# Slot sums in three pieces, row sums ahead of the second layer, and fewer half-width pieces at the end of a pooled-attention and soft-MoE kernel

## The chip, the cores and the metric

The kernel runs on one core of one Trainium2 chip. A core has TensorE (PE in the profile; its weight loads are PEld), VectorE (DVE), ScalarE (ACT), GpSimd (POOL) and SyncE (SP), which work side by side and wait for one another through semaphores, and 16 DMA engines that all queues share. The metric is the device time in microseconds; lower is better.

## The reference

Queries, keys and values have 8 batches, 8 heads, 576 tokens and 64 columns. Keys and values are averaged over 8 neighbouring tokens (72 remain), and ordinary softmax attention follows. Its output, 4608 tokens of 512 columns, goes through a soft mixture of 8 experts with 4 slots each:

```python
logits = x @ phi                       # 4608 x 32
d = softmax(logits, over the tokens)
slot_input = d.T @ x                   # 32 slots x 512
for e in range(E):
    h = np.maximum(slot_input[e] @ w1[e], 0.0)    # 4 x 1024
    slot_out[e] = h @ w2[e]                       # 4 x 512
c = softmax(logits, over the slots)
return c @ slot_out                    # 4608 x 512, float32
```

`w1` and `w2` have 16.8 MB each, the output has 9.4 MB. Both softmaxes use the same exponentials, divided once by sums over tokens and once by sums over slots.

## The kernel before

**Attention.** The batches go in four pairs. POOL issues all loads in an order written out by hand, and they are cast to bf16 on the way. For each pair the scores of a head are one `score_unit` (line 301): two matmuls into the bank pair `sc`, one exponential on ACT into `exa`. A `u_tile` (311) handles 128 tokens of four heads (one of two `qd`): its matmuls write the unnormalised attention output, the head's share of the logits and the row sum into `u_ps`; DVE inverts the sum (`rec`) and DVE, or ACT with `by_scalar`, writes the normalised result into `xsa`. A pair has nine such tiles (t = 0 to 8) for each `qd`. `u_ps` has two buffers, so the matmuls of a tile wait until the tile before last is normalised. Until the attention closes, a scheduler orders PE, ACT and DVE; only POOL's order is by hand. Behind `att.close()` (503) all engines follow the order of the code.

**Slot sums.** `dispatch` (334) sums the logits over heads (on PE with an identity, or on DVE for the last pair), takes the exponentials `ee` on ACT, and adds nine matmuls, one for each tile t, into `G_ps`. `add_up` adds the pairs into `G`, and for the last pair into `Gb`. `turn` (355) transposes the exponentials into `cT`, which the combination with the experts' outputs needs. For pairs 0 to 2 this lies beside the next pair's attention. For the last pair (lines 471 to 478) nothing is left beside it.

**Experts.** `hidden` (514) multiplies the slots with `w1` into `h_ps`, `turn_hidden` transposes `h` into `hT`. The inverse `recC` of the sums over tokens is made on DVE, and with it `hz`, `z_ps` and `zT`: a shortcut by which the very last row group of `w2` reaches the first two output tiles without waiting for `so`. `second_layer` (538) adds products of `hT` with row groups j = 0 to 7 of `w2` for each expert into `so_ps`. `row_sums` (403) computes the sums over slots as matmuls of `cT` with one-hot columns, copies them to SBUF on ACT, and turns them into `recR`. `busy(n)` (568) multiplies something that nobody reads (`idle_ps`).

**w2.** Experts 0 to 5 and row groups 0 to 2 of expert 6 are loaded in full width. The rest (13 row groups: five of expert 6, eight of expert 7) is loaded in column halves, first all left halves, then all right halves (487 to 495), into `xsa`, which the last pair's tokens leave free. `PIECES` (92) lists them.

**Output.** Tokens are written in groups of 2, 2, 2, 4, 6, 8 and 12 rows a partition (`GROUPS`, 57); a row is an output tile of 128 tokens. `begin(half)` (611) scales `so_ps` by `recC` into `so_a` and `so`, and makes tiles 0 and 1; `tiles` (624) makes more tiles of one half and stores them. Ten tiles are made by halves. The left half is done while the right half's weights still arrive. Tiles 10 to 35 are made in full width, ACT and DVE taking turns, and stored by whole groups through SP.

Of the kernel before, what the change touches and what calls it, by code (L numbers as in the profile page):

```python
# [18 lines left out]
def kernel(  # L19
# [36 lines left out]
    GROUPS, base = [], 0  # L56
    for rows in (2, 2, 2, 4, 6, 8, 12):
        GROUPS.append((rows, base))
        base += 128 * rows
# [28 lines left out]

    CUT6 = FJ - 5
    HC = DM // 2  # L90
# [219 lines left out]

    def u_tile(pair, qd, t, ex, by_scalar=False):

        ps = ps_u.tile([128, HQ, XW + 1], FP, name="u_ps", tag="u")
        for hh in range(HQ):
            for b in range(2):
                if t < 8 and b != t // 4:
                    continue
                c = (t % 4 if t < 8 else 4) * 128
                rows = slice(0, 128) if t < 8 else slice(b * 64, (b + 1) * 64)
                nc.tensor.matmul(out=ps[rows, hh],  # L320
                                 lhsT=ex[b][:, hh].rearrange("p r t -> p (r t)")[:, c:c + rows.stop - rows.start],
                                 rhs=vp[(2 * pair + b) % 5][:, qd * HQ + hh, 0:XW + 1],
                                 start=True, stop=True)
        rec = small.tile([128, HQ], FP, name="rec", bufs=3)
        nc.vector.reciprocal(out=rec, in_=ps[:, :, XW])  # L325
        dst = xs[pair][:, t, qd * HQ:(qd + 1) * HQ, :]
        if by_scalar:
            for hh in range(HQ):
                nc.scalar.activation(out=dst[:, hh], in_=ps[:, hh, 0:XW], func=AF.Copy, scale=rec[:, hh:hh + 1])
        else:  # L330
            nc.vector.tensor_tensor(out=dst, in0=ps[:, :, 0:XW],  # L331
                                    in1=rec.rearrange("p h -> p h ()").to_broadcast([128, HQ, XW]), op=ALU.mult)

    def dispatch(x, ps, ee, by_vector=False):

        if by_vector:
            lg = small.tile([128, 9, NS], FP, name="lg", bufs=1)
            nc.vector.reduce_sum(out=lg, in_=x[:, :, :, D:XW].rearrange("p t h c -> p t c h"), axis=AX.X)  # L338
        else:
            lg = ps_m.tile([128, 9, NS], FP, name="lg_ps", tag="m")  # L340
            for h in range(H):
                nc.tensor.matmul(out=lg, lhsT=ident, rhs=x[:, :, h, D:XW], start=(h == 0), stop=(h == H - 1))
        nc.scalar.activation(out=ee, in_=lg.rearrange("p t s -> p t () s").to_broadcast([128, 9, NG, NS]), func=AF.Exp)  # L343
        yield
        for t in range(9):
            nc.tensor.matmul(out=ps, lhsT=ee[:, t].rearrange("p g s -> p (g s)"), rhs=x[:, t, :, 0:D],  # L346
                             start=(t == 0), stop=(t == 8))
# [23 lines left out]
    def combine(pair):  # L371

        ps = ps_m.tile([128, DM], FP, name="G_ps", tag="m")
        ee = small.tile([128, 9, NG, NS], BF, name="ee", bufs=1)
        parts = dispatch(xs[pair], ps, ee)
        next(parts)
        yield
        next(parts, None)
        add_up(pair, ps, G)
# [19 lines left out]
    for c, (n, t) in enumerate(quads + rest):  # L399
        for i in range(2 * t.shape[1]):  # L400
            place[n + i] = (i, c)

    def row_sums():

        ps = ps_m.tile([NC, 4, 128], FP, name="R_ps", tag="m")
        for c, (_, t) in enumerate(quads + rest):
            nc.tensor.matmul(out=ps[:, 0:2 * t.shape[1]].rearrange("p (s r) i -> p s r i", r=2),   # L407
                             lhsT=onehot[:, MAXC - 1 - c:MAXC - 1 - c + NC], rhs=t,
                             start=(c == 0), stop=(c == NC - 1), skip_group_check=True)
        sums = consts.tile([NC, 4, 128], FP)  # L410
        nc.scalar.copy(out=sums, in_=ps)
        ps = ps_m.tile([128, 4, NC], FP, name="RT_ps", tag="m")
        for i in range(4):
# [24 lines left out]
    for pair in range(NP):  # L438
        for qd in range(2):
# [5 lines left out]
            for i in range(9):  # L445
# [5 lines left out]
                else:  # L451
                    u_tile(pair, qd, i - 5, ex)
                step(prep)
# [124 lines left out]
    so = post.tile([128, DM], BF)  # L578

    out_a = exf.rearrange("p (n c) -> p n c", c=DM)  # L580
    out_b = w1f.rearrange("p (n c) -> p n c", c=DM)
    n = 0
    places = []
    for rows, base in GROUPS:
        home = out_a[:, n:n + rows] if n + rows <= 6 else out_b[:, n - 6:n - 6 + rows]
        places.append((home, out[base:base + 128 * rows].rearrange("(p r) c -> p r c", r=rows)))
        n += rows
# [44 lines left out]
    for e in range(4):  # L632
        second_layer(e)
    row_sums()
    busy(512)
# [20 lines left out]
    tiles(4, 6, 1)  # L656
    tiles(6, 10, 1)
    for n in range(10, len(TILES)):
        g, r = TILES[n]
# [33 lines left out]
```

## Time and profile before

| | us |
|---|---|
| median of 3 runs (lowest, highest) | 175.68 (175.49, 175.91) |
| span of the profiled execution, first to last instruction | 179.6 |
| PE, DVE, ACT busy | 129.9, 97.1, 88.3 |
| last score exponentials end, `Gb` starts | 110.6, 128.59 |
| loads end, first store issued | 148.3, 152.40 |
| last store issued, landed | 167.5, 178.3 |

For the profiled execution only the span is given, with profiling running; the runs had none. A line of the chain of waits is one link of the work that ended last: start, duration, engine, tile written, line of code, count of instructions. A line of windows gives the busy time of each engine in one stretch, then the clock granted to TensorE (1.00 is full), the share of the 16 DMA engines, and the bytes moved. The share can pass 1, since packets overlap in the records.

### The profile page before, as it was taken

How to read it: one execution, taken by the hardware profiler on the slowest of the kernel's cores; microseconds unless marked ns; L12 is line 12 of the kernel's file. 1: busy time of each engine (PE TensorE's matmuls, PEld its weight loads, DVE VectorE, ACT ScalarE, POOL GpSimd, SP SyncE). 2: the span in 40 equal slices, each digit the busy share in tenths (PEclk: the TensorE clock that was granted, in tenths of full speed). 3: DMA queues.
4: the chain of work that ended last, by engine and by line, in shares of the span. 5: the costliest groups of instructions: out<-in, count | busy, mean ns of one | idle time of the engine just before them, and what ended most of it. 6: DMA issues, size and time to landing. Idle time of an engine off the chain costs nothing.

```text
span 179.6 us, 2853 instructions
## 1 busy us (share of the span) xinstructions
PE 129.9 (72%) x1106; PEld 70.2 (39%) x1106; DVE 97.1 (54%) x258; ACT 88.3 (49%) x168; POOL 19.9 (11%) x37
## 2 busy tenths in 40 slices
PE   0006888999899999999998996512996988798000
PEld 0002463565555655556555543300443232333000
DVE  5403353387868588785888629764335000599200
ACT  3201238986887649876599726232012012799100
POOL 7000111052100040000100004000700300000000
PEclk9999999999999999999999669655559999999755
DMA  5999999999999999999999999999999990699995
GB/s 197 242 209 233 207 220 216 213 224 203 204 220 216 216 207 220 225 204 219 208 230 204 221 217 210 228 206 223 214 210 207 196 181 7 225 342 428 480 394 235
DMA packets 10780, 41.13 MB, mean 229 GB/s; under 512 B 768, under 2 KB 6656, under 8 KB 7184
## 3 DMA queue, kind: packets, MB, share of 16 engines
q0 software_dynamic: 7440, 30.48, 83.9%
q1 hardware_dynamic: 3328, 10.49, 15.0%
q8 instruction: 8, 0.13, 0.3%
q14 instruction: 4, 0.03, 0.0%
HBM read 61.93 MB, written 9.44 MB: 397 GB/s over the span
## 4 chain that ended last, share of the span: by engine, by line
PE 51%; ACT 17%; DVE 14%; DMA 6%; issue 3%; POOL 1%; DVEq 0%; ACTq 0%; POOLq 0%
PE pool_ps L234 9%; ACT exa L308 7%; DMA phi_f<-in_moe_phi_dram 6%; PE G_ps L346 6%; PE sc L306 6%; PE u_ps L320 6%; PE q_ps L266 5%; DVE w_sb L575 4%; PE h_ps L521 3%; DVE xsa L331 3%; PE so_ps L542 3%; ACT vmeans L240 2%; DVE lg L338 2%; PE R_ps L407 2%; PE turn_ps L250 2%
## 5 line engine op out<-in xcount | busy, mean ns | idle before, releaser
L308 ACT ACTIVATE exa<-sc 72x576 bf16<-72x576 f32 x64 | 39.5, 652 | 5.1 <-PE sc L306 4.3
L331 DVE TENSOR_TENSOR xsa<-u_ps,rec 128x384 bf16<-128x384 f32 x69 | 37.4, 554 | 1.3
L320 PE MATMUL u_ps<-vp,exa 72*128 72x97 bf16 (+1 forms) x320 | 27.3, 217 | 4.5 <-DVE xsa L331 3.7
L320 PEld LDWEIGHTS <-exa 72*128 72x128 bf16 (+1 forms) x320 | 18.2, 104 | 16.0 <-DVE xsa L331 6.8
L306 PE MATMUL sc<-qTa,kp 64*72 64x288 bf16 x128 | 22.0, 309 | 1.9 <-ACT exa L308 1.5
L234 PE MATMUL pool_ps<-big,pmat 128*128 128x512 bf16 x64 | 18.6, 411 | 0.7 <-ACT qTa L270 0.6
L325 DVE RECIPROCAL rec<-u_ps 128x4 f32<-128x4 f32 x72 | 11.5, 172 | 12.8 <-PE u_ps L320 12.6
L346 PE MATMUL G_ps<-xsa,ee 128*128 128x512 bf16 x36 | 12.0, 496 | 6.6 <-ACT ee L343 6.6
L266 PE MATMUL q_ps<-ident,big 128*128 128x128 bf16 x144 | 12.5, 231 | 0.2
L186 PE MATMUL phi_ps<-spread,sel 128*128 128x256 bf16 x4 | 1.3, 397 | 15.1 <-DVE spread L181 15.1
L600 PE MATMUL f_ps<-so,cT 128*128 128x512 bf16 (+1 forms) x42 | 10.2, 337 | 1.8 <-ACT w_sb L573 0.8
L306 PEld LDWEIGHTS <-kp 64*72 64x72 bf16 x128 | 8.0, 108 | 8.3 <-issue 3.1
L575 DVE TENSOR_SCALAR w_sb<-f_ps,recR 128x512 f32<-128x512 f32 (+1 forms) x17 | 10.5, 683 | 0.4 <-PE f_ps L600 0.2
L266 PEld LDWEIGHTS <-big 128*128 128x128 bf16 x144 | 9.6, 104 | 2.4 <-issue 0.7
L242 DVE TENSOR_REDUCE rsum<-rest_ps 128x64 f32<-128x512 f32 x8 | 5.5, 692 | 9.3 <-PE rest_ps L238 9.2
L270 ACT COPY qTa<-q_ps 128x768 bf16<-128x768 bf16 x8 | 6.3, 794 | 7.8 <-PE q_ps L266 7.8
L272 DVE COPY qTa<-q_ps 128x768 bf16<-128x768 bf16 x16 | 8.8, 553 | 2.1 <-PE q_ps L266 2.0
L573 ACT ACTIVATE w_sb<-f_ps,recR 128x512 f32<-128x512 f32 (+1 forms) x17 | 9.6, 638 | 0.5 <-PE f_ps L600 0.3
L492 POOL DMA_DIRECT2D xsa<-in_moe_w_dram x8 | 6.0, 754 | 26.2 <-PE G_ps L346 15.3
L346 PEld LDWEIGHTS <-ee 128*128 128x128 bf16 x36 | 4.1, 120 | 12.3 <-ACT ee L343 6.8
L234 PEld LDWEIGHTS <-pmat 128*128 128x128 bf16 x64 | 5.8, 103 | 6.4 <-issue 2.3
L240 ACT CAST vmeans<-pool_ps 128x1024 bf16<-128x1024 f32 x4 | 4.0, 1012 | 6.8 <-PE pool_ps L234 6.8
(104 smaller groups left out, 155.1 us busy)
## 6 DMA issues: line engine op xcount, KB each, us to landing
w_sb<-in_moe_w_dram POOLq DMA_DIRECT2D x2, 3072.0 KB, 37.2
big<-in_q_dram POOLq DMA_DIRECT2D x4, 1152.0 KB, 12.0
big<-in_v_dram POOLq DMA_DIRECT2D x4, 1152.0 KB, 15.8
big<-in_moe_w_dram POOLq DMA_DIRECT2D x1, 4096.0 KB, 40.0
big<-in_k_dram POOLq DMA_DIRECT2D x3, 1152.0 KB, 21.4
out_dram<-w_sb SPq DMA_DIRECT2D x1, 3072.0 KB, 10.8
qTa<-in_moe_w_dram POOLq DMA_DIRECT2D x1, 2048.0 KB, 30.4
out_dram<-w_sb SPq DMA_DIRECT2D x1, 2048.0 KB, 7.5
```

The source lines that it names most:

```text
L234: nc.tensor.matmul(out=ps, lhsT=pmat, rhs=src[:, t:full * POOL:POOL, :], start=(t == 0), stop=(t == POOL - 1))
L266: nc.tensor.transpose(out=ps[:, t].rearrange("p n i -> p (n i)"), in_=q_sb[pair][:, tt:tt + 2, :].rearrange("p t d -> p (t d)"), identity= ...
L272: nc.vector.tensor_copy(out=dst, in_=ps)
L306: nc.tensor.matmul(out=ps[:, r, 0:S // 2], lhsT=kp[pair][rows, n], rhs=qT[pair][rows, n].rearrange("p t i -> p (t i)"), start=True, stop=True)
L308: nc.scalar.activation(out=dst.rearrange("p r (i t) -> p r i t", t=NU), in_=ps[:, :, 0:S // 2].rearrange("p r (t i) -> p r i t", i=NI), fu ...
L320: nc.tensor.matmul(out=ps[rows, hh], lhsT=ex[b][:, hh].rearrange("p r t -> p (r t)")[:, c:c + rows.stop - rows.start], rhs=vp[(2 * pair + ...
L325: nc.vector.reciprocal(out=rec, in_=ps[:, :, XW])
L331: nc.vector.tensor_tensor(out=dst, in0=ps[:, :, 0:XW], in1=rec.rearrange("p h -> p h ()").to_broadcast([128, HQ, XW]), op=ALU.mult)
L346: nc.tensor.matmul(out=ps, lhsT=ee[:, t].rearrange("p g s -> p (g s)"), rhs=x[:, t, :, 0:D], start=(t == 0), stop=(t == 8))
L573: nc.scalar.activation(out=dst, in_=src, func=AF.Copy, scale=by)
L575: nc.vector.tensor_scalar(out=dst, in0=src, scalar1=by, scalar2=None, op0=ALU.mult)
L600: nc.tensor.matmul(out=ps, lhsT=tokens(n), rhs=so[:, cols], start=True, stop=True)
```

## The change

1. For the last pair, the logits go through PE (`weigh`) and the slot sums (`gather`) in three pieces: tiles 0 to 3, 4 to 6 and 7 to 8. DVE's reduction of the logits is gone. Tiles 1, 3, 5 and 7 of the last half pair are normalised on ACT, where it was 4, 6 and 8. Tiles 6, 7 and 8 are written into the free score banks (`spare`) instead of `u_ps`.
2. `row_sums` is split: its ten matmuls and the copy move ahead of `z_ps`, and `turn_sums` with the inverses stays behind the first four experts. Three more `busy(512)` follow there.
3. `CUT6` goes from 3 to 7: seven row groups of expert 6 are loaded whole, and one of expert 6 and eight of expert 7 by halves.
4. `GROUPS` becomes 2, 2, 4, 6, 8, 14, and eight tiles are made by halves.

```diff
-    for rows in (2, 2, 2, 4, 6, 8, 12):
+    for rows in (2, 2, 4, 6, 8, 14):
...
-    CUT6 = FJ - 5
+    CUT6 = 7
...
-    def u_tile(pair, qd, t, ex, by_scalar=False):
-
-        ps = ps_u.tile([128, HQ, XW + 1], FP, name="u_ps", tag="u")
+    def u_tile(pair, qd, t, ex, by_scalar=False, ps=None):
+
+        if ps is None:
+            ps = ps_u.tile([128, HQ, XW + 1], FP, name="u_ps", tag="u")
...
-    def dispatch(x, ps, ee, by_vector=False):
-
-        if by_vector:
-            lg = small.tile([128, 9, NS], FP, name="lg", bufs=1)
-            nc.vector.reduce_sum(out=lg, in_=x[:, :, :, D:XW].rearrange("p t h c -> p t c h"), axis=AX.X)
-        else:
-            lg = ps_m.tile([128, 9, NS], FP, name="lg_ps", tag="m")
-            for h in range(H):
-                nc.tensor.matmul(out=lg, lhsT=ident, rhs=x[:, :, h, D:XW], start=(h == 0), stop=(h == H - 1))
-        nc.scalar.activation(out=ee, in_=lg.rearrange("p t s -> p t () s").to_broadcast([128, 9, NG, NS]), func=AF.Exp)
-        yield
-        for t in range(9):
+    def weigh(x, ee, t0, t1):
+
+        lg = ps_m.tile([128, t1 - t0, NS], FP, name="lg_ps", tag="m")
+        for h in range(H):
+            nc.tensor.matmul(out=lg, lhsT=ident, rhs=x[:, t0:t1, h, D:XW], start=(h == 0), stop=(h == H - 1))
+        nc.scalar.activation(out=ee[:, t0:t1], in_=lg.rearrange("p t s -> p t () s").to_broadcast([128, t1 - t0, NG, NS]),
+                             func=AF.Exp)
+
+    def gather(x, ps, ee, t0, t1):
+
+        for t in range(t0, t1):
             nc.tensor.matmul(out=ps, lhsT=ee[:, t].rearrange("p g s -> p (g s)"), rhs=x[:, t, :, 0:D],
                              start=(t == 0), stop=(t == 8))
...
-                    u_tile(pair, qd, i - 5, ex)
+                    u_tile(pair, qd, i - 5, ex, by_scalar=pair == NP - 1 and qd == 1 and i in (6, 8))
...
-    u_tile(*last[:2], 4, last[2], by_scalar=True)
+    x = xs[NP - 1]
     G_ps = ps_m.tile([128, DM], FP, name="G_ps", tag="m")
     ee = small.tile([128, 9, NG, NS], BF, name="ee", bufs=1)
-    for i in range(1, 5):
-        u_tile(*last[:2], 4 + i, last[2], by_scalar=i % 2 == 0)
-    for _ in dispatch(xs[NP - 1], G_ps, ee, True):
-        pass
+    wide = [ps_sc.tile([128, 2, 512], FP, name="sc") for _ in range(2)]
+    spare = [wide[i // 2][:, i % 2, 0:HQ * (XW + 1)].rearrange("p (h c) -> p h c", h=HQ) for i in range(3)]
+    for i in range(5):
+        u_tile(*last[:2], 4 + i, last[2], by_scalar=i % 2 == 1, ps=spare[i - 2] if i >= 2 else None)
+        if i == 2:
+            weigh(x, ee, 0, 4)
+    gather(x, G_ps, ee, 0, 4)
+    weigh(x, ee, 4, 7)
+    gather(x, G_ps, ee, 4, 7)
+    weigh(x, ee, 7, 9)
+    gather(x, G_ps, ee, 7, 9)
     add_up(NP - 1, G_ps, Gb)
...
     turn_hidden(1)
+    row_sums()
...
     for e in range(4):
         second_layer(e)
-    row_sums()
+    turn_sums()
+    busy(512)
+    busy(512)
+    busy(512)
     busy(512)
...
     tiles(2, 3, 0)
     tiles(3, 4, 0)
-    for n in (4, 6):
-        tiles(n, n + 2, 0)
+    tiles(4, 6, 0)
     for e, j0, j1 in PIECES[:2]:
         second_layer(e, j0, j1, 1)
-    tiles(8, 10, 0)
+    tiles(6, 8, 0)
...
-    tiles(6, 10, 1)
-    for n in range(10, len(TILES)):
+    tiles(6, 8, 1)
+    for n in range(8, len(TILES)):
```

How the instructions stand on three engines, before and then after (line numbers differ, since lines were added):

ACT, from the last tiles of the attention to the scaled half of the experts' output (`xsa` is a normalised tile of one head, `ee` the exponentials, `h_sb` the hidden layer, `sums` the row sums):

```order
L329 ACTIVATE xsa<-u_ps,rec 128x96 x12
L343 ACTIVATE ee<-lg 128x1152
L526 ACTIVATE h_sb_1719<-h_ps 128x512
L526 ACTIVATE h_sb_1720<-h_ps 128x512
L562 CAST zT<-z_ps 128x256
L411 COPY sums<-R_ps 10x512
L573 ACTIVATE so_a<-so_ps,recC 128x256
```

```order
L330 ACTIVATE xsa<-u_ps,rec 128x96 x8
L340 ACTIVATE ee<-lg_ps 128x512
L330 ACTIVATE xsa<-u_ps,rec 128x96 x4
L330 ACTIVATE xsa<-sc,rec 128x96 x4
L340 ACTIVATE ee<-lg_ps 128x384
L340 ACTIVATE ee<-lg_ps 128x256
L536 ACTIVATE h_sb_1749<-h_ps 128x512
L536 ACTIVATE h_sb_1750<-h_ps 128x512
L411 COPY sums<-R_ps 10x512
L573 CAST zT<-z_ps 128x256
L584 ACTIVATE so_a<-so_ps,recC 128x256
```

One exponential over 1152 columns became three, the first ahead of tiles 5 and 7, and the copy of the row sums moved ahead of `zT`.

PE, where the transposes of `h` end and the second layer begins:

```order
L533 LDWEIGHTS h_sb_1720
L533 MATMUL hT_ps<-ident,h_sb_1720 128x128
L560 LDWEIGHTS hz
L560 MATMUL z_ps<-cT,hz 128x256
L542 LDWEIGHTS hT
L542 MATMUL so_ps<-big,hT 32x512
```

```order
L408 LDWEIGHTS onehot
L408 MATMUL R_ps<-cT,onehot 10x256
L571 LDWEIGHTS hz
L571 MATMUL z_ps<-cT,hz 128x256
L552 LDWEIGHTS hT
L552 MATMUL so_ps<-big,hT 32x512
```

The row sums (`R_ps`) now stand between the transposes and `z_ps`. In the three pieces, PE's order behind the last `u_ps` tile is: four slot sums with the matmuls of tile 7 between the second and the third, eight logit matmuls, three slot sums, eight logit matmuls, two slot sums.

POOL, the last loads (`big`, `qTa` and `xsa` hold row groups of `w2`):

```order
L120 DMA qTa<-in_moe_w_dram 128x2x4096
L120 DMA xsa<-in_moe_w_dram 128x1536
L492 DMA xsa<-in_moe_w_dram 128x5x256
L492 DMA xsa<-in_moe_w_dram 128x4x256
L492 DMA xsa<-in_moe_w_dram 128x3x256
L492 DMA xsa<-in_moe_w_dram 128x256
```

```order
L120 DMA qTa<-in_moe_w_dram 128x2x4096
L120 DMA xsa<-in_moe_w_dram 128x3584
L502 DMA xsa<-in_moe_w_dram 128x256
L502 DMA xsa<-in_moe_w_dram 128x4x256
L502 DMA xsa<-in_moe_w_dram 128x3x256
L502 DMA xsa<-in_moe_w_dram 128x256 x2
```

Four row groups of expert 6 moved from the half-width pieces into the full-width load ahead of them.

More of the change, by code (lines that the diff above doesn't have):

```diff
@@ L374, in combine @@
         ee = small.tile([128, 9, NG, NS], BF, name="ee", bufs=1)
-        parts = dispatch(xs[pair], ps, ee)
-        next(parts)
+        weigh(xs[pair], ee, 0, 9)
         yield
-        next(parts, None)
+        gather(xs[pair], ps, ee, 0, 9)
         add_up(pair, ps, G)
@@ L401 @@
             place[n + i] = (i, c)
+    sums = consts.tile([NC, 4, 128], FP)
     def row_sums():
@@ L409, in row_sums, with turn_sums @@
                              start=(c == 0), stop=(c == NC - 1), skip_group_check=True)
-        sums = consts.tile([NC, 4, 128], FP)
         nc.scalar.copy(out=sums, in_=ps)
+    def turn_sums():
         ps = ps_m.tile([128, 4, NC], FP, name="RT_ps", tag="m")
@@ L578 @@
     so = post.tile([128, DM], BF)
+    IN_A = 8
     out_a = exf.rearrange("p (n c) -> p n c", c=DM)
@@ L584 @@
     for rows, base in GROUPS:
-        home = out_a[:, n:n + rows] if n + rows <= 6 else out_b[:, n - 6:n - 6 + rows]
+        home = out_a[:, n:n + rows] if n + rows <= IN_A else out_b[:, n - IN_A:n - IN_A + rows]
         places.append((home, out[base:base + 128 * rows].rearrange("(p r) c -> p r c", r=rows)))
```

## The prediction

> **What bounds the kernel now.** I read the profiled execution first for its length, then the chain of waits, then the windows of the last 30 us.
>
> ```profile
> span 179.6 us, 2853 instructions
> ```
>
> The median of the unprofiled runs is 175.68 us, 3.9 less than this span; no other time of the profiled execution is given. I work in the profile's clock and subtract the same microseconds from the median. A difference of 0.2% (0.35 us) is about the least that a measurement of this kernel tells from none.
>
> From the chain of waits (start, duration, engine, tile, line, count), the stretch behind the attention:
>
> ```profile
> 119.29 4.00 DVE lg L338
> 123.31 1.17 ACT ee L343
> ...
> 124.53 4.03 PE G_ps L346 x9
> ...
> 130.33 5.32 PE h_ps L521 x58
> ...
> 136.33 0.73 PE hT_ps L533 x8
> ...
> 138.53 0.28 PE z_ps L560
> 138.81 1.84 PE so_ps L542 x32
> 140.65 3.99 PE R_ps L407 x10
> ...
> 145.70 1.05 PE idle_ps L569 x2
> ...
> 151.07 0.48 ACT so_a L573
> ...
> 154.27 0.23 PE f_ps L600
> ...
> 154.53 0.49 DVE w_sb L575
> 155.03 0.46 ACT so_a L573
> ```
>
> One engine works at a time: the logits of the last pair wait for the last tile, the exponentials for all logits, the slot sums for all exponentials, and everything behind waits for the slot sums. Windows show what the memory does meanwhile (columns: stretch, length, busy time of PE, PE loads, DVE, ACT, POOL with counts, granted clock, DMA share, GB/s):
>
> ```profile
> 148.30:152.40 4.10, 3.74 (x26) 1.34 (x25) 0.21 (x1) 0.95 (x2) 0.00 (x0) 1.00 0.05 6
> 152.40:156.30 3.90, 2.94 (x26) 1.33 (x25) 2.21 (x6) 2.98 (x7) 0.00 (x0) 1.00 0.56 185
> 156.30:167.50 11.20, 8.89 (x35) 3.71 (x33) 10.62 (x18) 9.88 (x19) 0.00 (x0) 1.00 1.05 398
> 167.50:178.30 10.80, 0.00 (x0) 0.00 (x0) 0.00 (x0) 0.00 (x0) 0.00 (x0) 0.52 0.92 394
> ```
>
> The loads are over at 148.3; the DMA stands still for 4.1 us, is half used for 3.9 us, and from 156.3 to the end is full. So the end follows the moment at which stores fill the DMA, and the chain above sets that moment. The most that any change of this chain can win is the unused DMA time: 4.1 x 0.95 + 3.9 x 0.44 = 5.6 us.
>
> When the weights of the second layer arrive is the other limit. Issues with their times to landing (us):
>
> ```profile
> 109.07 0.58 POOL L120 DMA_DIRECT2D xsa<-in_moe_w_dram  x1
> ```
> ```profile
> xsa<-in_moe_w_dram POOLq DMA_DIRECT2D x1, 384.0 KB, 31.6
> ```
> ```profile
> L492 POOL DMA_DIRECT2D xsa<-in_moe_w_dram x2: 598/688/778, 126.6 to 127.4; - x2
> DMA to landing us min/median/max: 17.6/17.8/18.0
> ```
>
> The first rows of expert 6 land at 109.07 + 31.6 = 140.7, the last left-half piece at 127.4 + 17.6 = 145.0, six us before the first scaling by `recC` (151.07) can use it. Between them lie 832 KB in 4.3 us, 193 KB per us. Before the change the weights are not what is waited for.
>
> **The change part by part.**
>
> *Slot sums in pieces.* The 4.00 us reduction goes; logits, exponentials and slot sums run for tiles 0-3, 4-6 and 7-8. What is left behind the last tile are the pieces that need it. Their prices:
>
> ```profile
> L343 ACT ACTIVATE ee<-lg_ps x3: 1130/1130/1134, 59.1 to 101.5; 128x1152 bf16<-128x1152 f32 x3
> ```
> ```profile
> L329 ACT ACTIVATE xsa<-u_ps,rec x12: 332/340/349, 114.6 to 118.9; 128x96 bf16<-128x96 f32 x12
> ```
> ```profile
> 100.27 1.14 PE L342 MATMUL lg_ps<-xsa,ident 128*128 128x288 bf16 x4
> ```
> ```profile
> 60.79 1.95 PE G_ps L346 x9
> ```
>
> ACT: 0.34 us for 96 columns and 1.13 for 1152 give 0.75 ns a column, so 0.65, 0.56 and 0.46 us for 512, 384 and 256. A logit matmul of 288 columns takes 0.28 here, so one of 64 about 0.06. A slot-sum matmul takes 4.03/9 = 0.45 at the low clock, 1.95/9 = 0.22 at the full one. ACT evicts tiles 1, 3, 5 and 7 now, at four times 0.26 us a tile (four activations in 1.04, overlapped), with the 0.65 exponential between 3 and 5. Walking the orders of PE, ACT and DVE from 109 us with the measured durations, I place tile 1 on ACT at 112.8, tile 3 at 114.5, the first exponential at 116.0, tile 5 at 116.7, and tile 7, whose matmuls stand behind the first two slot sums, at 118.2. It ends at about 119.3, where the last tile ended before: DVE does fewer tiles, but ACT does its four in series. Bounds for that end: 117.6 (ACT never waits) and 120.3 (one more wait of a tile). Behind it: exponential of tiles 4-6 0.56, three slot sums 1.34, eight logits 0.48 (PE works in order, so they stand behind those three), exponential 0.46, two slot sums 0.90, hand-overs 0.4: 4.14. Before it was 128.56 - 119.29 = 9.27. **Gain 5.1**, bounds 6.8 and 0.4 (the second if nothing overlaps, worked out below). Reading from the score banks instead of `u_ps` I price like reading `u_ps`; no row shows it, the nearest (1130 from PSUM against 4.00 of DVE) gives no reason for more.
>
> *Row sums sooner.* They stand between the transposes of `h` (end 137.06) and `z_ps` (138.53), where PE waits 1.47 for DVE. One group has 14 rows a partition instead of 12, read in wider strides. The ten matmuls differ by that already:
>
> ```profile
> L407 PE MATMUL R_ps<-cT,onehot x10: 270/556/854, 140.5 to 144.3; 128*10 128x512 bf16 x8, 128*10 128x256 bf16 x2
> ```
>
> The wider ones are the slower; a seventh step on three matmuls and one extra half costs an estimated 0.5, bounds 0 and 1. So `z_ps` comes 3.99 + 0.5 - 1.47 = 3.0 later. Behind the 32 matmuls, 3.99 goes, and of the 1.06 between its end (144.64) and the filler (145.70) the copy with its hand-overs, an estimated 0.65, is covered. Three more fillers (`idle_ps`) cost 3 x 1.05 = 3.15. Together 3.0 - 3.99 - 0.65 + 3.15 = **a loss of 1.5**: the fillers eat what the moved sums free. It is a loss only as long as PE, and not a landing, is last.
>
> *Nine groups of w2.* Seven rows of expert 6 come whole (896 KB instead of 384), so the last left-half piece has 512 KB more before it and 256 KB less: 1088 KB behind 140.7, at 193 KB per us 146.3. POOL issues them earlier, since slot sums free `xsa` sooner, but lands them in the same order:
>
> ```profile
> L492 POOL DMA_DIRECT2D xsa<-in_moe_w_dram x8: 591/772/883, 109.6 to 141.2; - x8
> ```
>
> Issue is up to 30 us ahead of landing, so POOL's waits cost nothing. The first scaling comes at 151.07 - 5.1 + 1.5 = **147.5** by the chain, 1.2 behind the landing. The right-half pieces then shrink from 832 to 576 KB and land at about 149.3, with the first stores beside them. No row shows stores beside loads; between no cost and 1.4 (loads halved in speed from 147.9) I take none, since stores leave 44% of the DMA unused at that stage.
>
> *Eight tiles by halves.* Between the two scalings lie 155.03 - 151.07 = 3.96; one pair of half tiles (154.27 to 155.03, 0.76) goes: **gain 0.8**, bounds 0.5 and 1.0. The right half would be scaled at 150.6, behind its landing. SP loses three issues that nothing waited for. Two half tiles fewer leave 0.26 MB more for later, but 0.52 MB go in full rows:
>
> ```profile
> 159.00:160.00 1.00, 1.00 (x5) 0.37 (x4) 1.00 (x2) 1.00 (x3) 0.00 (x0) 1.00 1.03 338
> ```
>
> At 338 GB/s for half rows against 394 for whole ones the queue from there on is **0.3 longer**, bounds 0 and 0.6. The last store has 14 rows, issued about 4.7 us behind the eight-row one (0.33 a tile: 12 tiles now in 4.0); that one's 2 MB take 5.3, so the DMA stays full.
>
> Sum: -5.1 + 1.5 - 0.8 + 0.3 = -4.1. Span 175.5, median **171.6 us**.
>
> **The clock.** Windows of the tail:
>
> ```profile
> 110.00:113.00 3.00, 1.43 (x20) 0.85 (x20) 2.86 (x9) 0.61 (x2) 0.52 (x1) 1.00 1.03 216
> 114.00:118.00 4.00, 2.20 (x24) 1.44 (x22) 2.22 (x7) 2.07 (x8) 0.00 (x0) 0.50 1.07 225
> 130.00:133.60 3.60, 3.60 (x35) 1.39 (x37) 1.54 (x4) 0.00 (x0) 0.39 (x1) 0.50 1.01 212
> ```
>
> The granted clock falls to 0.50 behind a stretch in which PE was half busy without a long pause, and returns only after 3.3 us of unbroken `h` matmuls. So I price slot sums low and `h` as before. [...]
>
> **The rivals.**
>
> 1. *The clock is up behind the attention.* [...] Five slot sums save 5 x 0.23 = 1.2, and `h` 3.27 x 0.52 = 1.7. The chain would be ready at 144.6, so the landing at 146.3 decides: 1.2 better than forecast, 170.4. For it: slot sums now fill PE nearly without breaks from 117. Against it: the windows above.
> 2. *The chain is later.* `h` stays at the low clock to its end (2.05 us at full clock become 4.2, +2.2), or tile 7 ends a microsecond later. Gain 1.9 to 3: about 173.3. [...]
> 3. *The pieces run one behind another* and nothing is won, the one that ends slower. PE takes its queue in order, and tile 7's matmuls stand behind two slot sums that wait for ACT. Tile 7 at 120.3, then 24 logit matmuls 2.2, exponentials 1.67, nine slot sums 4.03, hand-overs 0.6: 128.8, 0.2 later than before; with +1.5 - 0.8 + 0.3 the time is 176.9. It decides from slot sums later than 127.5 on. Against it: the first six tiles need nothing of the last ones.
> 4. *The change does not do what it says*: row sums and fillers only swap places, and halves of tiles were never waited for. In part I forecast this: it is the loss of 1.5.
>
> **How the numbers follow.** Forecast 0.52 (its own range 170.9 to 172.6), rival 1 0.23, rival 2 0.18, rival 3 0.07 (of it 0.02 within 0.2%). Floor: 5.6 less gives 170.1, with shorter half-row stores 169.8. Leaving out rival 3 and the worst of rival 2: 169.8 to 174.0. Faster 0.93, same 0.02, slower 0.05.
>
> **What would show it.** Right: `Gb` starts at 123 to 124 with no DVE reduction before it; three `ee` activations; row sums straight behind the transposes of `h`; the first `so_a` near 147.5; DMA share without a gap between loads and stores. Wrong: `Gb` behind 127, PE waiting for a landing ahead of the first `so_a` (then rival 1), a clock of 0.50 through all of `h` (rival 2), or a dry DMA ahead of the last store.

## The result, and the profile after

| us | median | lowest to highest | runs | profiled span |
|---|---|---|---|---|
| before, on the same chip | 175.80 | 175.49 to 180.71 | 4 | 179.6 (shown ahead of the prediction) |
| after | 177.87 | 177.52 to 178.13 | 4 | 175.7 |

The change makes the kernel slower: after to before is 1.0117, 95% interval 1.0100 to 1.0135, about 2.1 us. The forecast was 171.6, its range 169.8 to 174.0, and 0.05 was given to slower. One thing has to be known to read these numbers: about a third of the executions of the kernel before are *long* (178.2 to 181.9 us) and the others *ordinary* (175.2 to 176.8), the profile that the prediction was made from is a long one, and all ratios here compare ordinary executions.

In every run of before and of the change the device time is the span plus 1.7 to 1.9 us (177.52 with a span of 175.7; 175.44 with 173.6; 180.73 with 178.9). So the execution with the span 179.6 took about 181.4 us, 5.7 more than the median 175.68, and the 3.9 us between that span and the median were not a cost of profiling. They came from comparing two different executions. The right profile to compare with is that of an ordinary execution of before (run e6 below, 175.44 us). Its page, and then the page of after: span, busy times, fetches of code (queue q8, count, MB), and the last store with its time to landing.

```profile
span 173.6 us, 2853 instructions
...
PE 123.7 (71%) x1106; PEld 67.7 (39%) x1106; DVE 97.0 (56%) x258; ACT 88.0 (51%) x168; POOL 19.9 (11%) x37
...
q8 instruction: 8, 0.13, 0.3%
...
out_dram<-w_sb SPq DMA_DIRECT2D x1, 3072.0 KB, 10.8
```

```profile
span 175.7 us, 2904 instructions
...
PE 127.8 (73%) x1130; PEld 70.0 (40%) x1130; DVE 92.4 (53%) x255; ACT 88.8 (51%) x173; POOL 19.2 (11%) x37
...
q8 instruction: 9, 0.15, 0.3%
...
out_dram<-w_sb SPq DMA_DIRECT2D x1, 3584.0 KB, 12.5
```

The chain of waits behind the attention, ordinary before and then after (start, duration, engine, tile, line, count):

```profile
115.09 4.00 DVE lg L338
119.11 1.17 ACT ee L343
120.33 4.03 PE G_ps L346 x9
124.39 0.69 DVE Gb L353
125.43 0.47 PE c_ps L361 x5
125.93 3.67 PE h_ps L521 x64
...
138.97 9.67 DMA xsa<-in_moe_w_dram
149.02 0.48 ACT so_a L573
```

```profile
112.16 0.61 ACT ee L340
112.81 1.05 PE G_ps L346 x2
114.14 0.51 POOL xsa L502
114.66 0.49 issue
115.16 30.15 DMA xsa<-in_moe_w_dram
145.68 0.48 ACT so_a L584
```

In the ordinary execution of before the chain already ends in a landing, the right-half weights at 148.64. After, it is in a landing from 115 to 145.31. PE shows the same from its side; the last column is its idle time and what ended it:

```profile
L353 DVE TENSOR_TENSOR Gb<-G,G_ps x1: 676/676/676, 119.1 to 119.1; 32x512 bf16<-32x512 f32 x1
```

```profile
138.39 1.05 PE L552 MATMUL so_ps<-qTa,hT 128*32 128x512 bf16 x16 [1.95 <-DMA qTa<-in_moe_w_dram]
...
142.66 0.61 PE L552 MATMUL so_ps<-xsa,hT 128*32 128x512 bf16 x7 [2.17 <-DMA xsa<-in_moe_w_dram]
...
145.35 0.29 PE L552 MATMUL so_ps<-xsa,hT 128*32 128x256 bf16 x3 [0.38 <-DMA xsa<-in_moe_w_dram]
```

`Gb` starts at 119.1 where it started at 124.39, so the slot sums did become 5.3 us sooner. PE then gives 1.95 + 2.17 + 0.38 = 4.5 us of it back in waits for weights. The first scaling comes at 145.68, 0.7 later than the 145.01 of before, and the last store leaves at 161.7 against 161.5. What is left of the 2.1 us lies behind that: the last landing takes 12.5 instead of 10.8.

### The profile page after: what moved, and what is told of

Same layout as the page of the kernel before. It is cut to its first block, busy times and chain, and to the rows that moved or that the text cites. A ratio compares the mean times of both kernels' runs of the same rounds, so it can differ in the third digit from the quotient of the medians.

```text
span 175.7 us, 2904 instructions
## 1 busy us (share of the span) xinstructions
PE 127.8 (73%) x1130; PEld 70.0 (40%) x1130; DVE 92.4 (53%) x255; ACT 88.8 (51%) x173; POOL 19.2 (11%) x37
## 4 chain that ended last, share of the span: by engine, by line
PE 36%; DMA 24%; ACT 18%; DVE 8%; issue 3%; POOL 1%; DVEq 0%; ACTq 0%; POOLq 0%
DMA xsa<-in_moe_w_dram 17%; PE pool_ps L234 9%; ACT exa L308 8%; DMA phi_f<-in_moe_phi_dram 7%; PE sc L306 6%; PE u_ps L321 5%; PE q_ps L266 5%; DVE w_sb L586 4%; PE G_ps L346 4%; ACT vmeans L240 2%; PE lg_ps L339 2%; ACT kmeans L240 2%; PE turn_ps L250 2%; ACT cT L366 1%; ACT vp L298 1%
## 5 line engine op out<-in xcount | busy, mean ns | idle before, releaser
L332 DVE TENSOR_TENSOR xsa<-u_ps,rec 128x384 bf16<-128x384 f32 x66 | 35.8, 553 | 1.2
L321 PE MATMUL u_ps<-vp,exa 72*128 72x97 bf16 (+1 forms) x304 | 25.8, 214 | 2.0 <-DVE xsa L332 1.2
L266 PE MATMUL q_ps<-ident,big 128*128 128x128 bf16 x144 | 11.6, 219 | 0.8 <-DVE qTa L272 0.2
L346 PE MATMUL G_ps<-xsa,ee 128*128 128x512 bf16 x36 | 10.5, 427 | 1.8 <-ACT ee L340 1.7
L266 PEld LDWEIGHTS <-big 128*128 128x128 bf16 x144 | 8.7, 97 | 2.9 <-issue 1.3
L586 DVE TENSOR_SCALAR w_sb<-f_ps,recR 128x512 f32<-128x512 f32 x14 | 9.3, 744 | 0.1
L502 POOL DMA_DIRECT2D xsa<-in_moe_w_dram x8 | 5.3, 660 | 33.0 <-DMA big<-in_moe_w_dram 12.2
L586 DVE TENSOR_SCALAR so<-so_ps,recC 128x256 bf16<-128x256 f32 x2 | 1.0, 484 | 14.7 <-PE so_ps L552 14.7
L584 ACT ACTIVATE w_sb<-f_ps,recR 128x512 f32<-128x512 f32 x14 | 8.4, 688 | 0.2
L584 ACT ACTIVATE so_a<-so_ps,recC 128x256 bf16<-128x256 f32 x2 | 0.9, 470 | 14.4 <-PE so_ps L552 14.4
## 6 DMA issues: line engine op xcount, KB each, us to landing
out_dram<-w_sb SPq DMA_DIRECT2D x1, 3584.0 KB, 12.5
```

Of the source, the lines that this page charges most:

```text
L266: nc.tensor.transpose(out=ps[:, t].rearrange("p n i -> p (n i)"), in_=q_sb[pair][:, tt:tt + 2, :].rearrange("p t d -> p (t d)"), identity= ...
L321: nc.tensor.matmul(out=ps[rows, hh], lhsT=ex[b][:, hh].rearrange("p r t -> p (r t)")[:, c:c + rows.stop - rows.start], rhs=vp[(2 * pair + ...
L332: nc.vector.tensor_tensor(out=dst, in0=ps[:, :, 0:XW], in1=rec.rearrange("p h -> p h ()").to_broadcast([128, HQ, XW]), op=ALU.mult)
L584: nc.scalar.activation(out=dst, in_=src, func=AF.Copy, scale=by)
L586: nc.vector.tensor_scalar(out=dst, in0=src, scalar1=by, scalar2=None, op0=ALU.mult)
```

## The experiments

**Is the profile that was read a usual execution? (e1, e5, e6.)** The kernel before, unchanged, in three single runs.

> The kernel before, unchanged, for a second look at its profile. The changed kernel's runs took 1.8 us more than their spans, so a run of 175.7 should have a span near 174.0, not the 179.6 of the profile I worked from. Theory 'landing' (the chain behind the attention was never last in an ordinary execution): the span is near 174, the first so_a starts at 145 to 146, right behind the landing of the last left-half piece, and the clock is up through most of the slot sums and h. Rival 'chain' (the first profile is typical): a span of 179 to 180 and the first so_a near 151.

> The kernel before once more, for a profile with a span near 174 (both profiles so far have 179 and the clock at 0.50 from 113 to 133 us). Theory 'clock' (the short executions of before are those in which the granted clock stays up behind the attention): clock 1.00 in most of 113 to 133, first so_a at 145.3 to 146.0, last store issued near 161.5 and landed near 172. Theory 'transfers' (something in the loads or stores is faster): first so_a anywhere, loads over before 147 instead of 148.3.

> As the look before it: the same kernel, so that one of the two is likely to be a short execution. A span of 178 or more shows the first so_a behind 149, one under 175 ahead of 147.

Measured: 180.73, 180.85 and 175.44 us, spans 178.9, 179.0 and 173.6. The third is the ordinary execution shown above. Windows of the two kinds (stretch, length, busy PE, PEld, DVE, ACT, POOL, granted clock, DMA share, GB/s), first the long one that the prediction used, then the ordinary one:

```profile
100.00:104.00 4.00, 4.00 (x21) 1.89 (x21) 1.83 (x5) 3.10 (x5) 0.00 (x0) 0.50 1.08 227
...
128.00:132.00 4.00, 3.82 (x36) 1.87 (x38) 2.26 (x6) 0.00 (x0) 1.62 (x2) 0.50 1.06 223
```

```profile
100.00:104.00 4.00, 3.99 (x35) 2.07 (x34) 2.21 (x7) 2.19 (x5) 0.00 (x0) 1.00 1.04 219
...
124.00:128.00 4.00, 3.62 (x55) 2.04 (x57) 2.95 (x7) 0.06 (x1) 0.63 (x1) 0.95 0.99 207
...
148.00:150.00 2.00, 1.57 (x15) 0.56 (x10) 0.72 (x2) 1.36 (x4) 0.00 (x0) 1.00 0.80 255
150.00:152.00 2.00, 1.45 (x11) 0.86 (x11) 1.50 (x4) 1.71 (x5) 0.00 (x0) 1.00 1.04 348
```

The same code meets a clock of 0.50 or 1.00 at 100 to 104 us, and again at the `h` matmuls. The attention then ends 4.2 us sooner (DVE's reduction starts at 115.09 instead of 119.29) and `h` takes 3.67 instead of 5.32. Together that moves the first scaling from 151.07 to 145.01. Theory 'clock' was not right in full: it expected 1.00 in most of 113 to 133, but in e6 the nine slot sums still took 4.03, as in the long execution. The left-half weights that the first scaling needs landed at 144.2, the last ones at 144.7, and the right half at 148.64, so an ordinary execution has next to nothing to win from a shorter chain.

**Is it the clock? (e7.)** Eleven matmuls that nobody reads keep TensorE busy while DVE reduces the logits.

```diff
+    keep = ps_m.tile([128, DM], FP, name="keep_ps", tag="m")
+    for _ in range(11):
+        nc.tensor.matmul(out=keep, lhsT=ident, rhs=xs[NP - 1][:, 8, :, 0:D], start=True, stop=True)
     for _ in dispatch(xs[NP - 1], G_ps, ee, True):
```

> The kernel before with eleven extra matmuls of 512 columns that read the last normalised tile and write a bank nobody reads, so that TensorE works during the 4 us reduction on VectorE. Nothing else is changed. Theory 'clock': the clock comes up before or in the slot sums, the slot sums take 2.0 instead of 4.0 us and h 3.6 instead of 5.3, so that no run is as long as 178 and all lie at 175 to 176.5. Theory 'transfers': the same mix of runs near 175.5 and near 180.5 as before.

Measured: 176.02 (175.38 to 177.22, 10 runs), ratio 1.0021 [0.9990, 1.0052]. None of the 10 runs was long; of the runs of before beside them 4 of 13 were. The mean over all runs is 176.2 against 177.4. The profiled one met the low clock at 100 to 104 and still recovered:

```profile
100.00:104.00 4.00, 4.00 (x20) 1.77 (x19) 1.48 (x4) 2.54 (x4) 0.00 (x0) 0.50 1.05 221
...
120.00:124.00 4.00, 3.47 (x10) 1.03 (x9) 2.64 (x1) 1.16 (x1) 0.00 (x0) 0.61 1.05 221
124.00:128.00 4.00, 3.54 (x31) 1.84 (x33) 1.91 (x5) 0.00 (x0) 2.97 (x4) 1.00 1.04 217
```

Its reduction starts late, at 118.63, as in a long execution, but the slot sums take 2.13 instead of 4.03 and `h` 3.67 instead of 5.32, which gives 3.5 us back. So the idle TensorE behind the attention is a large part of what makes a long execution long; the rest goes with the early low clock, behind which the reduction starts 3.5 us later (118.63, in e6 115.09). It is no full cure: with the same matmuls and other output groups (e15 below) 3 of 12 runs were long.

**One part of the change at a time (e2, e3, e4).** e2 is the changed kernel with the old output groups and ten half tiles, e3 the changed kernel with `CUT6` = 3, e4 the kernel before with the slot sums in pieces alone.

```diff
# e2, against the changed kernel
-    for rows in (2, 2, 4, 6, 8, 14):
+    for rows in (2, 2, 2, 4, 6, 8, 12):
# e3, against the changed kernel
-    CUT6 = 7
+    CUT6 = FJ - 5
# e4, against the kernel before
-    for _ in dispatch(xs[NP - 1], G_ps, ee, True):
-        pass
+    gather(x, G_ps, ee, 0, 4)
+    weigh(x, ee, 4, 7)
+    gather(x, G_ps, ee, 4, 7)
...
```

> The changed kernel with the output groups of before (2, 2, 2, 4, 6, 8, 12; ten tiles by halves); all else as changed. Theory 'stores' (the 14-row last store and the earlier end of the half tiles lengthen the way from the first so_a to the end, 30.0 us in the changed kernel): 1.3 to 1.8 us less than the changed kernel, 176.0 to 176.6. Theory 'landing of w2' (the left halves come later by the four whole rows): no more than 0.4 from the changed kernel's 177.9.

> The changed kernel with three whole row groups of expert 6 again (13 half-width groups); all else as changed. Theory 'landing of w2': the first so_a comes about 1.2 us sooner (256 KB fewer ahead of it at 193 to 210 KB per us), near 144.5, and the time is about 176.7. Theory 'stores': so_a sooner too, but the stores then run beside more loads and the end does not move: 177.5 to 177.9.

> The kernel before with the slot sums in three pieces alone (logits on PE, ACT tiles 1, 3, 5, 7, spare score banks). Theory 'landing': the chain gets ready some microseconds sooner, but the landing decides, so within 0.4 us of before, 175.3 to 176.1. Rival 'chain': 5 us less than before, near 170.7.

Measured: 178.14 (ratio 1.0127 [1.0072, 1.0182]), 178.08 (1.0118 [1.0045, 1.0191]), 177.97 (1.0111 [1.0065, 1.0158]). Undoing the groups or the cut wins nothing, and the pieces alone cost as much as the whole change. In the profile of e4 the pieces do their work:

```profile
121.91 1.05 PE G_ps L346 x2
122.99 0.69 DVE Gb L353
...
124.73 5.96 PE h_ps L527 x64
...
146.10 0.48 ACT so_a L579
```

```profile
q8 instruction: 9, 0.15, 0.3%
...
out_dram<-w_sb SPq DMA_DIRECT2D x1, 3072.0 KB, 12.3
```

The attention ends late there, as in a long execution, and `Gb` comes at 122.99 (128.59 in the long before). But `h` takes 5.96 at the low clock, and the last 3072 KB need 12.3 us to land instead of 10.8. The page also has a ninth fetch of code on queue q8. In the window from 155 to 157 us of the changed kernel, in the middle of the stores, it stands beside them:

```profile
q1 hardware_dynamic: 126, 0.80, 99.5%
q8 instruction: 1, 0.02, 2.9%
```

**Does the ninth fetch cost the time? (e8, e9, e10.)** e8 and e9 are the kernel before with 20 and 100 one-column matmuls at the start, where PE has nothing to do. They were meant to change nothing but the count and the place of the fetches of code. e10 is the changed kernel with two pieces (tiles 0 to 4 and 5 to 8) and without the three new fillers, 14 matmuls fewer in the records.

```diff
# e8 (range(100) in e9), against the kernel before
+    for _ in range(20):
+        nc.tensor.matmul(out=pad[:, 0:1], lhsT=ident, rhs=zeros[:, 0:1], start=True, stop=True)
# e10, against the changed kernel
-            weigh(x, ee, 0, 4)
-    gather(x, G_ps, ee, 0, 4)
-    weigh(x, ee, 4, 7)
-    gather(x, G_ps, ee, 4, 7)
-    weigh(x, ee, 7, 9)
-    gather(x, G_ps, ee, 7, 9)
+            weigh(x, ee, 0, 5)
+    gather(x, G_ps, ee, 0, 5)
+    weigh(x, ee, 5, 9)
+    gather(x, G_ps, ee, 5, 9)
...
-    busy(512)
-    busy(512)
-    busy(512)
```

> The kernel before with 20 matmuls of one column at the very start, where TensorE waits for data anyway; nothing reads them. It has 1126 matmuls instead of 1106 (the changed kernel 1130, the kernel with the pieces alone 1130, the one with eleven extra matmuls 1117). Theory 'code fetch': beyond some 1117 matmuls TensorE's code needs a ninth block of 16 KB, which comes through one DMA engine between 150 and 158 us, in the middle of the stores; that engine's part of every later store lands about 1 us behind the others. So 9 records of the instruction queue instead of 8, the last store landing 11.8 to 12.5 us behind its issue instead of 10.8, and 1.0 to 1.5 us more than before: 176.6 to 177.1. Rival 'pieces' (the work of the pieces itself costs it): no change, 175.4 to 176.0.

> As the kernel with 20 extra matmuls, but with 100, so that the ninth block is fetched about 80 matmuls earlier in the work, near 138 to 142 us, while loads and not stores run (a tenth would need some 1245 matmuls; there are 1206). Theory 'code fetch' (it is the place in the stores that costs): 9 records, none behind 146 us, last store 10.8 to 11.2 us to landing, time 175.4 to 176.2. If the number of blocks alone costs, or matmuls at the start do: 176.6 or more, as with 20.

> The changed kernel with two pieces (tiles 0 to 4, 5 to 8) instead of three and without the three extra fillers: 1116 matmuls instead of 1130; all else as changed. Theory 'code fetch': 8 records, last store (14 rows) landing about 11.4 us behind its issue instead of 12.5, and 1.0 to 1.4 us less than the changed kernel: 176.5 to 176.9. What is left over before is the later landing of the left halves. Rival 'pieces': 177.5 to 178.0 as changed.

Measured: e8 177.42 (ratio 1.0073 [1.0036, 1.0109]), e9 1.0038 [0.9997, 1.0078], e10 176.87 (1.0046 [1.0027, 1.0066]). Pages of e8, e9 and e10:

```profile
q8 instruction: 9, 0.15, 0.3%
...
out_dram<-w_sb SPq DMA_DIRECT2D x1, 3072.0 KB, 12.5
```

```profile
q8 instruction: 9, 0.15, 0.3%
...
out_dram<-w_sb SPq DMA_DIRECT2D x1, 3072.0 KB, 10.8
```

```profile
q8 instruction: 8, 0.13, 0.3%
...
out_dram<-w_sb SPq DMA_DIRECT2D x1, 3584.0 KB, 11.3
```

Twenty tiny matmuls at the start of the kernel lengthen the last landing by 1.7 us and the time by 1.3. The ninth fetch falls between 155 and 158 us, among the stores, and takes 1.7% of 16 engines in the 4 us from 155, 1.1 us of one engine. The packets of the change, which has a ninth fetch there too, show what follows: the fetch is one packet of 16 KB, from 155.53 us on, which takes 0.92 us on one of the 16 DMA engines. The packets that stand behind it end to end run on to 173.8, while all others of the last store end by 172.7, 1.2 us sooner. With 100 of them the ninth fetch falls at 145.7, ahead of the stores (the first leaves at 149.14), and the last landing is 10.8 again: for the landing the place counts, not the number. (That rests on the landing. The time of e9 says less: 7 of its 12 runs were long, for a reason that stays open, and of the five others one, 178.14, lies between the two kinds.) e10 has no ninth fetch among the stores and is 1.0 us faster than the change (1.2 by the ratios). Between two fetches lie 113 to 137 matmuls with their weight loads in the change, 125 in the mean, and the ninth comes behind the 1116th of its 1130.

**The pieces without the later landing (e11).** e10 with `CUT6` = 3 and without the two fillers of 256 columns.

> As the one with two pieces, and with three whole row groups of expert 6 as before (13 half-width groups), and without the two short fillers, which keeps it at 1116 matmuls. Theory 'landing of w2': the first so_a starts 0.6 to 0.8 us sooner, near 144.9, and the time is 175.4 to 176.2, with none of the executions of 180. If so_a is sooner and the end is not, the stores decide, at 176.5 to 177.

Measured: 177.78 (177.38 to 179.66, 6 runs), 1.0102 [1.0044, 1.0159], 0.9 above e10 although the first scaling comes at 144.8. Windows:

```profile
148.00:150.00 2.00, 1.73 (x12) 0.37 (x7) 0.48 (x1) 1.00 (x3) 0.00 (x0) 0.50 0.99 317
...
152.00:154.00 2.00, 2.00 (x8) 0.92 (x6) 1.42 (x4) 1.83 (x5) 0.00 (x0) 0.50 0.41 134
```

The clock is at 0.50 from 144 to 154 here, the output tiles come slower, and the DMA is only 0.41 used from 152 to 154. The low clock begins at 137.9, near the end of a wait of 5.0 us in which TensorE has nothing to do until weights land at 138.4. But e10 has nearly the same wait (5.3 us), its clock falls at 138.4, and it is back at 145.2. e10 has the two fillers of 256 columns that e11 leaves out, so e11 does not tell whether the old cut or the missing fillers kept the clock down, and it does not show what the old cut is worth.

The profiled executions of e2 (0.50 from 150 to 154) and e3 (0.54 to 0.61 from 150 to 154) have a low clock in the output too. It does not explain their times: other runs of e2 and e3, with a granted clock of 0.923 and 0.930 in the mean against 0.881 to 0.902 in e11, took as long (177.79 to 178.11). Both still have the ninth fetch among the stores, and e2 keeps the cut, e3 the groups.

**The other parts alone (e12, e13, e14), and two of them with the matmuls of e7 (e15, e16).** Each is the kernel before with one part: e12 `CUT6` = 7, e13 the groups with eight half tiles, e14 the row sums ahead of `z_ps` with three fillers. e15 is e13, and e16 is e12, each with the eleven matmuls of e7.

> The kernel before with CUT6 = 7 alone: seven row groups of expert 6 whole, nine groups in halves; slot sums, row sums and output groups as before. About 0.8 us of the 2.1 by which the change is slower is still without a place. Theory A (the later landing of the left halves costs it): the first `so_a` moves from 145.0 to between 145.7 and 146.6 and waits for a landing, and the time is 176.2 to 176.6, 0.5 to 0.8 above before. Theory B (the wider last group costs it, not the landing): 175.7 to 175.9, no difference. The matmuls stay 1106, so no ninth code fetch among the stores. As recorded in the prediction, the left half lands 1.3 us later and, in executions that are limited by the landing, the first scaling with it.

> The kernel before with the output groups 2, 2, 4, 6, 8, 14 and eight tiles by halves alone; slot sums, row sums and loads as before. Theory A (the landing of the left halves costs the remaining 0.8 us): 175.4 to 175.8, no difference or 0.3 better. Theory B (the last group of 14 rows is issued no earlier and has 0.5 MB more behind it, and too little is queued ahead of it): last store issued within 0.5 of 161.5, landing 11.3 to 12 instead of 10.8, time 176.2 to 176.8. The prediction priced this part at -0.8 + 0.3 = -0.5 us.

> The kernel before with the row sums ahead of `z_ps` and three more fillers of 512 columns alone. The prediction priced this at a loss of 1.5 us on the chain. In ordinary executions the chain and the landing of the left halves meet (first `so_a` 145.0, landing 144.9), so if the price is right the first `so_a` comes at 146.5 and the time rises by 0.5 to 1.5, to 176.2 to 177.2. If the moved row sums and the fillers cancel on the path: first `so_a` within 0.4 of 145.0 and 175.7 to 175.9. The matmuls rise to about 1112, still short of the ninth fetch among the stores.

> The new output groups with eight half tiles alone, as in e13, but with the eleven matmuls of e7 that keep TensorE busy through the reduction, so that no execution is long. What e13 showed in one ordinary execution (the DMA is only 0.62 used from 152 to 154 us, and the last store leaves 0.6 later and lands 0.5 later) should stand in all runs: 176.7 to 177.2, 1.0 above the 176.0 of e7. If e13's execution was an accident: 175.8 to 176.2. The prediction had -0.5 for this part.

> CUT6 = 7 alone, as in e12, with the same eleven matmuls. If the later landing of the left half costs time of its own: 176.5 to 177.0, and in the profile the first `so_a` at 145.7 to 146.5 behind a landing. If the loads are only reordered and the DMA is full either way: 175.8 to 176.2, no difference from e7.

Measured:

| run | part | ratio to before |
|---|---|---|
| e12 | cut | 1.0022 [0.9978, 1.0066] |
| e13 | groups | 1.0096 [1.0010, 1.0183] |
| e14 | row sums, fillers | 1.0014 [0.9966, 1.0061] |
| e15 | groups, matmuls of e7 | 1.0063 [1.0038, 1.0088] |
| e16 | cut, matmuls of e7 | 1.0039 [1.0005, 1.0072] |

The groups cost 0.7 to 1.1 us by themselves. e15 carries this: its nine ordinary runs have a median of 176.71, against 175.74 of before beside it and 176.02 of e7. e13 carries little, since five of its six runs were long (why so many stays open) and its ratio counts one of them, 179.08, beside its only ordinary run, 176.52. That one was profiled, so it can be laid beside e6. First e6, its stores (durations of the issue in ns, starts of first and last), one window and the row sums in the chain, then e13:

```profile
L591 SPq DMA_DIRECT2D out_dram<-w_sb x6: 332/388/564, 149.3 to 161.5; - x6
```

```profile
152.00:154.00 2.00, 2.00 (x9) 0.85 (x9) 1.87 (x4) 2.00 (x5) 0.00 (x0) 1.00 1.02 335
```

```profile
134.59 3.99 PE R_ps L407 x10
```

```profile
L592 SPq DMA_DIRECT2D out_dram<-w_sb x3: 332/344/345, 154.8 to 162.1; - x3
```

```profile
152.00:154.00 2.00, 2.00 (x9) 0.76 (x8) 1.86 (x5) 2.00 (x5) 0.00 (x0) 1.00 0.62 207
```

```profile
134.49 4.61 PE R_ps L407 x10
```

With eight half tiles the six-row store, the first in full width, leaves at 154.8 as before (154.9), and less is queued ahead of it: the DMA is 0.62 used for 2 us where it was full. The missing 0.26 MB move to the end. The last store leaves 0.6 later and lands 0.5 later (11.3 for 10.8), which is the 1.1 between the spans 174.7 and 173.6. (Single ordinary executions of before differ by as much, 175.15 to 176.81, so the pair shows the mechanism and e15 the size.) The changed kernel has the same gap, 0.75 of the DMA in that window:

```profile
152.00:154.00 2.00, 2.00 (x8) 0.81 (x8) 1.86 (x4) 2.00 (x5) 0.00 (x0) 1.00 0.75 249
```

Not all of it need be the store queue. The row sums of the 14-row group take 4.61 instead of 3.99, and the first store of e13 leaves 0.5 later (146.86 for 146.34). How the loss divides between the two was not measured.

For the cut, e16's profile shows a landing in front of the first scaling:

```profile
122.64 22.96 DMA xsa<-in_moe_w_dram
```

It ends at 145.6, where the same weights landed at 144.2 in e6; the scaling comes at 146.0, 1.0 later than there. The time rises by 0.7 against before, but only by 0.4 against the 176.02 of e7, which the interval does not tell from nothing. e14 shows no difference that its four ordinary runs can tell (interval -0.6 to 1.1 us).

The parts add up only roughly. The ninth fetch (1.3 in e8, 1.0 to 1.2 from e10 to the change) and the groups (0.7 to 1.1) make 1.7 to 2.4, beside the measured 2.1. Without the fetch, e10 is 0.8 above before (1.0046). With 0.4 to 0.7 of the cut the sum comes to 2.1 to 3.1, so at its upper end the cut would have to share its time with the groups: the later first scaling and the thin queue at 152 would both leave the DMA short ahead of the full-width stores. That sharing is argued and was not measured. No kernel with the two pieces, the old groups, the old cut and no ninth fetch was run, so whether the pieces have any value beside e7's eleven matmuls stays open.

## Why the prediction was wrong

**What bounds the kernel now: the step that failed.** "The end follows the moment at which stores fill the DMA, and the chain above sets that moment" held for the execution that was read. There the loads were over at 148.3 and the DMA stood still for 4.1 us. In the ordinary one loads run to about 148.6 and the first store leaves at 146.34. The DMA is 0.80 used from 148 to 150 and full from 150 on, so about 0.4 us are unused there. The 5.6 us from which the whole gain was to come do not exist. The sign to see was in the prediction's first lines. A span 3.9 us longer than the median was taken as a clock to subtract in, though a constant cost of profiling was only assumed. The times, 175.49 to 175.91, could not show the long executions, but a span above all of them could.

**Slot sums in pieces, a gain of 5.1.** The size is right and the place is wrong. `Gb` came 5.6 sooner against the long execution (e4) and 5.3 against the ordinary one (after). Of this the first scaling saw 5.0 in an execution with the early low clock (151.07 to 146.10) and nothing in an ordinary one, where the landing decides. The pieces seem to work on what made the long executions long: over 179 us were 3 of the 34 runs of the kernels with pieces (the highest 181.37, in e3), and 27 of 90 runs of before. The term that the sum lacked is the code itself: 24 more matmuls in the records bring a ninth fetch among the stores, 1.0 to 1.3 us.

**Row sums sooner, a loss of 1.5.** The sign is right and the size too high. Measured in e14 from the first transpose of `h` to the last product ahead of the first scaling: 132.49 to 148.28, against 135.55 to 150.96 in the long before, 15.8 against 15.4, so 0.4. Without the 14-row group the prediction's terms give 1.0. The fillers cost 2.6 for three and not 3.15, since one next to another they take 0.86. The 0.5 for the wider group was near (4.61 instead of 3.99 in e13). It came out as it was qualified: no loss once a landing is last. In the change the fillers do another thing that no term had: TensorE waits 1.95 us there for the weights in `qTa` and its clock stays at 1.00, while in e10, without them, it waits 5.3 us and the clock falls to 0.50 for 6.8 us.

**Nine groups of w2.** The last left-half piece, forecast 1.3 later at 146.3, landed at 145.7 in the change and 146.0 in e16, against 144.7 in e6: 1.0 to 1.3 later, so this term is right. The piece ahead of it, for which the first scaling waits, landed at 145.3 and 145.6, against 144.2. "Stores beside loads at no cost" was priced at a stage that an ordinary execution does not have.

**Eight tiles by halves, a gain of 0.8 and 0.3 longer stores.** Between the two scalings lie 3.33 us (149.01 - 145.68), 0.7 less than the 4.01 of the ordinary before. That this is close to 0.8 is luck. In e6 the second scaling waits for the right-half weights (148.64), and with the groups alone (e13) it waits for them too and comes at 149.30, no sooner than the 149.02 of e6. Where no landing is last, the pair of half tiles is worth 0.5 (3.43 in e15, 3.95 in e7), the lower bound. The sentence that failed is "so the DMA stays full". It was worked out for the last store. Ahead of the six-row store nobody looked, and there the DMA runs short (0.62 in e13, 0.75 in the change). Instead of -0.5 the part costs 0.7 to 1.1.

**The clock and the rivals.** In the change the clock is up from 120 us on (the first slot sums still meet 0.50, 1.05 us for two), `h` takes 3.64, and the landing decides: the mechanism of rival 1, nearly with its clock and with its landing, but not its 170.4. Rival 2's slow `h` is e4 (5.96). Rival 3 was the one that was to end slower; it did not happen. What did happen, fuller code and a thin store queue, was no rival at all. Before's reduction leaves TensorE 6.6 us without a matmul in e6 (113.8 to 120.3), and where e7 fills this the clock is back by 124, against 133.6 in the long before (but 124.4 in e6, which does not fill it). In e6 the clock was at 0.50 from 108 to 112 us already, with PE busy for 2.64 of 4 us and no pause above 0.7 us between 104 and 112. So the long pause did not lower it there; what did, no run shows.

**The chances.** 0.93 on faster rested on the forecast and rivals 1 and 2, which all took the same bound. None of them asked whether that bound was there in the executions that the median counts.

## What to carry to other kernels

Before working in the clock of a profiled execution, set its span against the times of the runs: if the time is not the span plus the offset that other runs show (here 1.8 us), the execution is of another kind, and its slack may not exist in the one that counts. When a stage is full of transfers, ask of every edit how much is queued just ahead of each store, and how many instructions it adds, since a fetch of code goes through the same DMA engines (0.92 us of one of them for 16 KB in the change). The cheapest thing found here is the eleven idle matmuls of e7: no gain in ordinary executions, but 176.2 instead of 177.4 in the mean of all runs (10 against 13).

## What was not expected of the hardware

- Twenty matmuls of one column each, put where TensorE had nothing to do, cost 1.3 us at the other end of the kernel (e8): a ninth fetch on the instruction queue falls among the stores, and the last store lands 12.5 us behind its issue instead of 10.8. In the change such a fetch, 16 KB, takes 0.92 us on one DMA engine, and that engine's share of a 16-engine store ends 1.2 us behind the others' (173.8, 172.7). A hundred of them leave the landing at 10.8, and their time is not told from before (1.0038 [0.9997, 1.0078]).
- The same program on the same core runs 175.44 or 180.85 us, and the traces differ in when TensorE's clock falls and returns (granted 1.00 or 0.50 at 100 to 104 us). Up to 140 us the stretches at 0.50 last 17.1 us in e6, 6.8 and 20.5 us in the long before, and 10.2 us in the change; what sets their start and their length was not shown. Between the two times lie 5.4 us, 3%: in the long before the attention ends later (the reduction starts at 119.29, in e6 at 115.09) and `h` takes longer (5.32, in e6 3.67), in a chain in which one engine works at a time.
